# Attention and two MLPs on one core: attention units of blocks 3 to 7 eight ticks earlier, and the sums of x earlier in their cycle

## The chip, the cores and the metric

The program runs on one core of one Trainium2 chip. The metric is device time in microseconds (us) of a whole execution, inputs and outputs in HBM; a shorter time is better. Matrix products run on TensorE (PE), elementwise work on VectorE (DVE), ScalarE (ACT) and GpSimd (POOL). Most transfers are issued by SyncE (SP), in the order in which they are written.

## The reference

Linear attention with softmax over the features of q and over the sequence of k, then two MLPs without biases, all in float32.

```python
batch, heads, seq, dim = 8, 8, 576, 64      # 4608 tokens, d_model 512, d_ff 2048
q_s = softmax(q, axis=-1); k_s = softmax(k, axis=seq)
kv = einsum('bhsd,bhde->...', k_s, v)       # one 64 x 64 matrix for each head
x = einsum('bhsd,bhde->bhse', q_s, kv)      # then put in rows of 512 = heads x dim
h = x @ w_in;  x = (h * sigmoid(h)) @ w_out           # first MLP
h = x @ w_in2; out = (h * clip(h + 3, 0, 6) / 6) @ w_out2   # second MLP
```

## The kernel before

**Blocks, cycles, ticks.** Each MLP works on 9 blocks of 512 tokens: blocks 0 to 7 are the first 512 tokens of batches 0 to 7, block 8 is the 64 that are left of each batch. The hidden layer is cut in 8 chunks of 256 columns, so a block has 8 cycles, p = 0 to 7, and a cycle has 8 ticks, k = 0 to 7. `cycle(g)` writes one cycle of the first MLP for blocks 1 to 8 (g = 8 n + p): products 1 and 5, 6, 2 and 3, 7, then 4 of the block's operands with the chunk's weights, by a scheme with 7 products in place of 8, and between them the matmuls of the second layer for the chunk before (`G(0)` to `G(7)`, tiles y). Matmuls in float32r take a high and a low part of each operand, three to a product (L78 to L80). The weights of the first layer are read back from HBM into a ring of two tiles, 1.75 MB a cycle (L285).

**What DVE does in a cycle.** It adds `s2` (L780), which product 7 waits for; finishes A (L785) and B (L790, which product 4 waits for); forms the gate (L628) and the low part of its result (L75). On top come the attention's steps.

**Attention.** A batch has 4 units of two heads. The units of batch b are worked on beside block b - 1, by a table of ticks: `x_at(u)` is the tick of the unit's output x, and the list `plan` has all other steps at fixed distances: -28 `at_soft` (two DVE reductions, L374 and L377, then a POOL add, L379), -21 `at_spread` and `at_shift` (small transfers by SP), -20 `at_norm` (L421 to L424), -12 `at_tadd` and `at_sub` (POOL, L348 and L404), -4 `at_tmul` (POOL, L356), -3 and -1 the cast and the low part of q (L364, L368), -6 `at_kv` (five matmuls into bank D, then L482 on DVE), 0 and 2 the two halves of x (three matmuls each into bank D, which ACT copies into x at L514 and L516). Units are 16 ticks, two cycles, apart: the cycles with x alternate with those with kv.

**Operands of the next block.** When x of the next block is complete, `sums_x` (L549) forms four differences in two parts of two; in the last cycle, p = 7, `operand_x` splits seven operands, each a cast by ACT (L583) and a subtraction by DVE (L585). x lies in the tile xr, one buffer, of which `x_raw(n)` takes a new tile for each block. Block 8 has its x in the tile `rest`.

The order on each engine is the order in which the code is written (`manual_schedule`); the framework adds the waits.

Of the kernel before, what the change touches and what calls it, by code (L numbers as in the profile page):

```python
# [8 lines left out]
F32 = mybir.dt.float32  # L9
# [8 lines left out]
P = 128  # L18
NP = H // 2
TB = 512  # L20
NB = NT // TB
NF = DFF // P
KC = DM // P
# [6 lines left out]
NC = NF // 2  # L30
# [6 lines left out]
def attention_two_mlps(ctx: ExitStack, tc: tile.TileContext, kqT, kv5, qn, w1, w2, out):  # L37
# [7 lines left out]
    def stack(name, bufs, st, **kw):  # L45
        return st.enter_context(tc.tile_pool(name=name, bufs=bufs, reuse_waits="tile", **kw))

    tokens, weights_1, sums, attn = (ctx.enter_context(ExitStack()) for _ in range(4))
    x_p = stack("x", 1, tokens)
# [243 lines left out]
    def turned(u):  # L293
        return u >= TURNED * NP
# [227 lines left out]
    xr = {}  # L522
    tx = {}

    def x_raw(n):
        if n == NB - 1:
            return rest
        if n not in xr:
            xr[n] = x_p.tile([P, KC, TB], F32, tag="xr", name="xr")
        return xr[n]  # L530

    def first_x(c):
        k = c // 2
# [7 lines left out]
    def sums_x(n, part, add=nc.vector):  # L541
        x = x_raw(n)
        b11, b12, b21, b22 = (x[:, 2 * k:2 * k + 2, j * HT:(j + 1) * HT] for k in range(2) for j in range(2))
        if part == 0:
            t = z_p.tile([P, 2, 2, HT], F32, tag="z3", name="tx")
            tx[n] = t[:, 0], t[:, 1], z_p.tile([P, 2, HT], F32, tag="t4", name="t4")
        t3, t2, t4 = tx[n]
        for o, a, b in (((t3, b22, b12), (b12, b12, b11)), ((t2, b22, b12), (t4, b21, t2)))[part]:
            add.tensor_tensor(out=o, in0=a, in1=b, op=ALU.subtract)  # L549
# [129 lines left out]
    def at(tick, fn, *args):  # L679
        events.setdefault(tick, []).append((fn, args))  # L680

    def x_at(u):
        b, c = divmod(u, NP)
        return 22 + 10 * c if b == 1 else 64 * (b - 1) + 16 * c + 4

    for u in range(NP, NU):
        x = x_at(u)
        before = x_at(u - 2) if u - 2 >= NP else None
        if before is None:
            at(-90, at_load, u)  # L690
            at(-90, at_load_ev, u)
        elif turned(u):
            at(max(x - 42, 0 if turned(u - 2) else before - 11), at_load, u)
            at(x - 36, at_load_ev, u)
            at(x - 32, at_load_t, u)
        else:
            at(before - 5, at_load, u)
            at(before - 5, at_load_ev, u)
        if turned(u):
            plan = [  # L700
                (-28, at_soft), (-27, at_kexp), (-26, at_sendnm), (-26, at_send, "qm"), (-25, at_qexp),
                (-21, at_shift), (-21, at_spread, "qm"), (-20, at_knorm), (-20, at_norm), (-18, at_send, "qr"),
                (-12, at_tadd), (-12, at_sub), (-11, at_spread, "qr"), (-10, at_texp), (-9, at_exp),
                (-4, at_tmul), (-3, at_tcast), (-1, at_tlow),
            ]
        else:
            plan = [
                (-18, at_soft), (-17, at_kexp), (-15, at_qexp), (-14, at_trk, 0), (-13, at_knorm), (-13, at_norm),
                (-12, at_trk, 1), (-8, at_trq, 0), (-7, at_trq, 1),
            ]  # L710
        plan += [(-6, at_kv), (-4, at_kvsplit), (0, at_xhalf, 0), (2, at_xhalf, 1)]
        for d, fn, *args in plan:
            at(x + d, fn, u, *args)
# [9 lines left out]
    def cycle(g):  # L723
        A, B_, C = (banks[k] for k in "ABC")
        lo, hi = slice(0, HT), slice(HT, TB)
        m, t, p = place(g)
        n = m * NB + t
        last = p == NC - 1
        G = lambda k: layer_out(g - 1, k)
        late = g >= LATE  # L730
        early = n == 1 and NC - 4 <= p < NC - 2

        cast_out = split_out(0, p, lambda: raw_out[p])

        def side(k):

            run(8 * g + k)
            if n == 1:
                if early and k == 2:
                    pre.append(prepare_in(p + 2))  # L740
                if k < 2:
                    cast_out[k][1]()
                for i in {0: (3, 5), 1: (6,)}.get(k, ()):
                    if len(pre) and p in (NC - 3, NC - 2):
                        pre[0][i][1]()
                        if i == 6:
                            pre.pop(0)
                if early and k in (2, 3, 5, 6):
                    pre[-1][{2: 0, 3: 1, 5: 2, 6: 4}[k]][1]()
            if late and g > LATE and k < 4:  # L750
                pump({NC - 1: (1.2, 0.8, 0.8, 0), 0: (1.2, 1.2, 1.2, 0.7)}.get(p, (1.2, 1.2, 1.2, 1.2))[k], keep=True)
            if p == NC - 2 and k in (6, 7):
                sums_x(n + 1, k - 6)
            if last:
                for i in {1: (1,), 3: (5,), 4: (6, 2), 5: (3,), 6: (7,), 7: (4,)}.get(k, ()):
                    operand_x(n + 1, i)

        if g == LATE:
            attn.close()
            kept_p[1] = stack("kept1", 1, kept, side="right")  # L760
            m2_p.append(stack("m2", 1, right, side="right"))
            order = [*(q for q in range(NC) if q != STAYS), STAYS]
            stream.extend((1, q, 0) for q in order)
            feed(2)
            steps.extend(chain([second(q, 0) for q in order]))
        if g == PER - 1:
            pump(99)
            right.close()
            keep_in(3, 4, 4)
        product(g, 1, A[:, lo], True)  # L770
        nc.scalar.copy(B_[:, lo], A[:, lo])
        product(g, 5, C[:, lo], True)
        s5 = z_p.tile([P, HT], F32, tag="s5", name="s5")
        nc.scalar.copy(s5, C[:, lo])
        side(0)
        G(0)
        G(1)
        product(g, 6, B_[:, lo], False)
        s2 = z_p.tile([P, HT], F32, tag="s2", name="s2")
        nc.vector.tensor_tensor(out=s2, in0=B_[:, lo], in1=s5, op=ALU.add)  # L780
        side(1)
        product(g, 2, A[:, lo], False)
        product(g, 3, A[:, hi], False)
        G(2)
        nc.vector.tensor_tensor(out=A[:, hi], in0=A[:, hi], in1=s2, op=ALU.add)  # L785
        ba, bc = bend(g, 0, A), bend(g, 1, B_)
        next(ba)
        side(2)
        product(g, 7, B_[:, lo], False)
        nc.vector.tensor_tensor(out=B_[:, hi], in0=B_[:, lo], in1=s5, op=ALU.add)  # L790
        next(ba)
        G(3)
        side(3)
        G(4)
        product(g, 4, B_[:, lo], False)
        if not early:
            load_w(g + 2)
        for _ in ba:
            pass
        next(bc)  # L800
        next(bc)
        side(4)
        G(5)
        for _ in bc:
            pass
        side(5)
        G(6)
        side(6)
        G(7)
        side(7)  # L810
# [519 lines left out]
```

## Time and profile before

| what | value |
| --- | --- |
| median of 3 runs | 1656.68 us (1655.41 to 1660.07) |
| the profiled execution's own time | 1654.42 us |
| its span, first to last instruction | 1652.6 us |
| busy share: PE, weight loads, DVE, ACT, POOL | 97%, 88%, 72%, 46%, 15% |
| DMA traffic over the span | 382.95 MB, mean 232 GB/s |

The span lies 1.8 us under the execution's own time, and that time 2.3 us under the median of the runs. A busy PE is not a PE at its peak, since its matmuls are pipelined and their ends are modelled; a wait shows more surely in the length of a cycle, which is taken here from one first matmul of product 1 to the next. The first MLP's block 2 starts at 259.31, block 3 at 354.04, block 4 at 451.13, block 5 at 547.15, block 6 at 643.23 and block 7 at 736.89 us from the start of the span.

### The profile page before, as it was taken

The page shows a single profiled execution, that of the slowest core. Times are in us where ns is not written, and L with a number is a line of the kernel's source. Part 1 is how long each engine was busy: PE and PEld are TensorE (multiplying, and loading weights), DVE is VectorE, ACT ScalarE, POOL GpSimd, SP SyncE. Part 2 cuts the span into 40 slices and gives each one's busy share as a digit, 9 for nine tenths or more (in the row PEclk, how much of TensorE's full clock was granted, in tenths as well). Part 3 has the DMA queues.
Part 4 walks back from the last instruction along what each step waited for, and adds up shares of the span by engine and source line. Part 5 has one row for each costly group of instructions (what it writes and reads, how often), then busy time and mean ns, then how long its engine had stood idle before and what let it go on. Part 6 is the DMA issues. An engine that isn't in the chain of part 4 may idle for free.

```text
span 1652.6 us, 28084 instructions
## 1 busy us (share of the span) xinstructions
PE 1607.8 (97%) x11112; PEld 1450.8 (88%) x11112; DVE 1191.6 (72%) x1910; ACT 766.7 (46%) x1383; POOL 251.6 (15%) x188
## 2 busy tenths in 40 slices
PE   6999999999999999999999999999999999999998
PEld 4445878888889888898889999999999999999998
DVE  6999687575656657557777677777776587777775
ACT  5444555454544545444444555555554343333332
POOL 2211232221322222200000222222220000000000
PEclk9999999999999999999999999999999999999999
DMA  8589989999999999958897955555557943333332
GB/s 292 181 287 304 254 231 235 264 275 253 215 308 257 230 266 255 237 206 309 315 364 291 359 203 204 200 202 206 198 204 285 381 156 128 128 128 128 135 122 76
DMA packets 89419, 382.95 MB, mean 232 GB/s; under 512 B 21832, under 2 KB 25928, under 8 KB 67400
## 3 DMA queue, kind: packets, MB, share of 16 engines
q1 hardware_dynamic: 77128, 321.66, 62.5%
q10 hardware_dynamic: 12160, 59.51, 9.8%
q8 instruction: 87, 1.43, 0.4%
q14 instruction: 44, 0.36, 0.1%
HBM read 282.07 MB, written 99.06 MB: 231 GB/s over the span
## 4 chain that ended last, share of the span: by engine, by line
PE 67%; DVE 16%; DMA 9%; ACT 4%; issue 3%; POOL 0%; ACTq 0%; SPq 0%; DVEq 0%; POOLq 0%
PE M L1086 20%; PE y L78 5%; PE y L79 5%; PE y L80 5%; PE B L78 4%; PE B L79 4%; PE B L80 4%; PE A L78 4%; PE A L80 4%; PE A L79 4%; DMA ring<-wd 3%; DMA gd<-g 2%; DMA gt<-gd 1%; PE C L80 1%; PE C L79 1%
## 5 line engine op out<-in xcount | busy, mean ns | idle before, releaser
L1086 PE MATMUL M<-kout,f 128*128 128x256 f32 x2268 | 272.6, 281 | 0.9 <-DVE f L987 0.9
L1086 PEld LDWEIGHTS M<-kout,f 128*128 128x128 f32 x2268 | 270.4, 189 | 1.5 <-DVE f L987 1.1
L78 PE MATMUL y<-gs,woh 128*128 128x512 f32 x512 | 204.8, 400 | 0.0
L79 PE MATMUL y<-gs,woh 128*128 128x512 f32 x512 | 202.4, 395 | 0.0
L80 PE MATMUL y<-gs,wol 128*128 128x512 f32 x512 | 200.2, 391 | 0.0
L985 ACT CAST f<-gt 128x1024 fp32r<-128x1024 f32 x72 | 75.6, 1050 | 180.2 <-DVE gt L960 103.4
L78 PE MATMUL B<-o,ring 128*128 128x256 f32 x492 | 142.4, 289 | 13.6 <-DVE s L780 7.2
L75 DVE TENSOR_TENSOR gs<-g,gs 128x512 fp32r<-128x512 f32 x128 | 101.5, 793 | 62.4 <-ACT gs L74 61.8
L80 PE MATMUL B<-o,ring 128*128 128x256 f32 x492 | 139.1, 283 | 0.0
L79 PE MATMUL B<-o,ring 128*128 128x256 f32 x492 | 139.0, 283 | 0.0
L626 ACT ACTIVATE g<-A 128x512 f32<-128x512 f32 x72 | 43.0, 598 | 182.9 <-DVE A L785 166.2
L78 PE MATMUL A<-op,ring 128*128 128x256 f32 x444 | 126.7, 285 | 0.4 <-DMA ring<-wd 0.3
L79 PE MATMUL A<-op,ring 128*128 128x256 f32 x444 | 125.4, 282 | 0.4 <-DVE op L585 0.4
L80 PE MATMUL A<-op,ring 128*128 128x256 f32 x444 | 125.4, 282 | 0.0
L78 PEld LDWEIGHTS B<-o,ring 128*128 128x128 f32 x492 | 93.1, 189 | 33.7 <-DVE s L780 12.7
L74 ACT CAST gs<-g 128x512 fp32r<-128x512 f32 x128 | 79.1, 618 | 79.3 <-DVE g L628 76.7
L80 PEld LDWEIGHTS y<-gs,wol 128*128 128x128 f32 x512 | 96.5, 189 | 21.7
L987 DVE TENSOR_TENSOR f<-gt,f 128x1024 fp32r<-128x1024 f32 x72 | 88.0, 1222 | 30.7 <-ACT f L985 29.4
L78 PEld LDWEIGHTS y<-gs,woh 128*128 128x128 f32 x512 | 97.1, 190 | 12.7
L79 PEld LDWEIGHTS y<-gs,woh 128*128 128x128 f32 x512 | 97.3, 190 | 8.7
L78 PE MATMUL B<-o,kin 128*128 128x256 f32 x324 | 93.2, 288 | 7.3 <-DVE B L871 7.2
L854 DVE SCALAR_TENSOR_TENSOR g<-a,A 128x512 f32<-128x512 f32 x72 | 49.5, 688 | 69.2 <-ACT a L847 59.8
(228 smaller groups left out, 4210.0 us busy)
## 6 DMA issues: line engine op xcount, KB each, us to landing
ring<-wd SPq DMA_DIRECT2D x66, 1792.0 KB
gd<-g SPq DMA_DIRECT2D x72, 512.0 KB
gt<-gd SPq DMA_DIRECT2D x36, 1024.0 KB
st<-w_dram SPq DMA_DIRECT2D x16, 1024.0 KB
st<-w_dram ACTq DMA_DIRECT2D x16, 1024.0 KB
ev<-kv_dram SPq DMA_DIRECT2D x24, 640.0 KB
wd<-ring ACTq DMA_DIRECT2D x8, 1792.0 KB
kout<-wd SPq DMA_DIRECT2D x6, 1792.0 KB
```

What stands on the lines that cost most here:

```text
L74: nc.scalar.copy(hi, src)
L75: nc.vector.tensor_tensor(out=lo, in0=src, in1=f32(hi), op=ALU.subtract)
L78: nc.tensor.matmul(o, lhsT=wh, rhs=xh, start=start, stop=False, **kw)
L79: nc.tensor.matmul(o, lhsT=wh, rhs=xl, start=False, stop=False, **kw)
L80: nc.tensor.matmul(o, lhsT=wl, rhs=xh, start=False, stop=stop, **kw)
L626: nc.scalar.activation(out=a, in_=hb, func=AF.Tanh, scale=0.5)
L854: nc.vector.scalar_tensor_tensor(out=x["g"][:, j], in0=x["a", j], scalar=1.0, in1=x["AB"[j]], op0=ALU.min, op1=ALU.mult)
L985: nc.scalar.copy(o[0], src)
L987: nc.vector.tensor_tensor(out=o[1], in0=src, in1=f32(o[0]), op=ALU.subtract)
L1086: nc.tensor.matmul(M[:, h * 2 * P:(h + 1) * 2 * P], lhsT=a, rhs=b, start=p == 0 and h == 0 and e == 0, stop=p == NC - 1 and e == 2, skip_g ...
```

## The change

The units of batches 3 to 7 move 8 ticks, one cycle, earlier, and all their steps with them (`x_at`); those of batches 1 and 2 stay. The last unit's x is then written in cycle 5 and no longer in cycle 6, and the first unit's x of the batch after falls in the last cycle of the block before it. That needs x of two blocks in the tile xr at once, so `x_raw` hands out one tile throughout, and waits on it are by its regions. The sums of x go from ticks 6 and 7 of cycle 6 to ticks 2 and 5, in blocks 2 to 8; in block 1 they stay. Two loads get lower bounds, so that they do not come before their buffer is free.

```diff
     def x_raw(n):
         if n == NB - 1:
             return rest
-        if n not in xr:
-            xr[n] = x_p.tile([P, KC, TB], F32, tag="xr", name="xr")
-        return xr[n]
+        if not xr:
+            xr[0] = x_p.tile([P, KC, TB], F32, tag="xr", name="xr")
+        return xr[0]
...
-        return 22 + 10 * c if b == 1 else 64 * (b - 1) + 16 * c + 4
+        return 22 + 10 * c if b == 1 else 64 * (b - 1) + 16 * c + (4 if b == 2 else -4)
...
             at(max(x - 42, 0 if turned(u - 2) else before - 11), at_load, u)
-            at(x - 36, at_load_ev, u)
-            at(x - 32, at_load_t, u)
+            at(max(x - 36, before - 4), at_load_ev, u)
+            at(max(x - 32, before), at_load_t, u)
...
-            if p == NC - 2 and k in (6, 7):
-                sums_x(n + 1, k - 6)
+            if p == NC - 2 and k in ((6, 7) if n == 1 else (2, 5)):
+                sums_x(n + 1, int(k > 2 + 4 * (n == 1)))
```

**DVE at the end of block 3.** Before, from the end of cycle 6 into cycle 7: the four sums (L549, tiles tx, xr, t), the two reductions of a unit (L374, L377), then the cycle's own L780.

```order
L628 SCALAR_TENSOR_TENSOR g<-g,B 128x512
L75 TENSOR_TENSOR gs<-g,gs 128x512
L549 TENSOR_TENSOR tx<-xr 128x512
L549 TENSOR_TENSOR xr<-xr 128x2x256
L549 TENSOR_TENSOR tx<-xr 128x512
L549 TENSOR_TENSOR t_3935<-xr,tx 128x512
L374 TENSOR_REDUCE nm<-k 128x1
L377 TENSOR_REDUCE qm<-q 96x12
L780 TENSOR_TENSOR s_3978<-B,s_3956 128x256
L585 TENSOR_TENSOR op_1022<-xr,op_1022 128x512
L785 TENSOR_TENSOR A<-A,s_3978 128x256
L790 TENSOR_TENSOR B<-B,s_3956 128x256
```

Of the change, the same place from cycle 6's L780 on:

```order
L780 TENSOR_TENSOR s_3882<-B,s_3860 128x256
L785 TENSOR_TENSOR A<-A,s_3882 128x256
L549 TENSOR_TENSOR tx<-xr 128x512
L549 TENSOR_TENSOR xr<-xr 128x2x256
L790 TENSOR_TENSOR B<-B,s_3860 128x256
L628 SCALAR_TENSOR_TENSOR g<-g,A 128x512
L75 TENSOR_TENSOR gs<-g,gs 128x512
L628 SCALAR_TENSOR_TENSOR g<-g,B 128x512
L75 TENSOR_TENSOR gs<-g,gs 128x512
L549 TENSOR_TENSOR tx<-xr 128x512
L549 TENSOR_TENSOR t_3916<-xr,tx 128x512
L482 SCALAR_TENSOR_TENSOR kv<-D,kr,mask 128x128
```

Two sums now stand between L785 and L790 of cycle 6, the other two after its last L75; the reductions have gone to the start of cycle 6, and in their place at the start of cycle 7 stands the other unit's normalisation (L414 to L424).

**DVE in cycle 4 of block 1.** Before, from the normalisation of one unit on (wol and wi are weights that are still being prepared):

```order
L421 TENSOR_REDUCE qs<-q 96x12
L423 TENSOR_SCALAR qs<-qs 96x12
L424 RECIPROCAL qr<-qs 96x12
L780 TENSOR_TENSOR s_1594<-B,s_1562 128x256
L251 TENSOR_TENSOR wol<-wo,woh 128x1024
L785 TENSOR_TENSOR A<-A,s_1594 128x256
L192 TENSOR_TENSOR s<-wi 128x256
L192 TENSOR_TENSOR s<-s,wi 128x256
L790 TENSOR_TENSOR B<-B,s_1562 128x256
```

Of the change:

```order
L421 TENSOR_REDUCE qs<-q 96x12
L423 TENSOR_SCALAR qs<-qs 96x12
L424 RECIPROCAL qr<-qs 96x12
L374 TENSOR_REDUCE nm<-k 128x1
L377 TENSOR_REDUCE qm<-q 96x12
L780 TENSOR_TENSOR s_1599<-B,s_1561 128x256
L251 TENSOR_TENSOR wol<-wo,woh 128x1024
L785 TENSOR_TENSOR A<-A,s_1599 128x256
L192 TENSOR_TENSOR s<-wi 128x256
L192 TENSOR_TENSOR s<-s,wi 128x256
L790 TENSOR_TENSOR B<-B,s_1561 128x256
```

The two reductions of batch 3's first unit stand in cycle 4 now, ahead of L780; they stood at the start of cycle 5.

**PE at the end of cycle 6 of block 1.** Before, the second half of x of batch 2's last unit (L78 to L80 into D) and then G(7):

```order
L78 MATMUL D<-qh,kh 128x320
L79 MATMUL D<-ql,kh 128x320
L80 MATMUL D<-qh,kl 128x320
L78 MATMUL y_1199<-gs,woh 128x512
L79 MATMUL y_1199<-gs,woh 128x512
L80 MATMUL y_1199<-gs,wol 128x512
```

Of the change:

```order
L78 MATMUL D<-qh,kh 128x320
L79 MATMUL D<-ql,kh 128x320
L80 MATMUL D<-qh,kl 128x320
L473 MATMUL D<-ev 128x128 x4
L474 MATMUL D<-ev 128x128
L78 MATMUL y_1198<-gs,woh 128x512
L79 MATMUL y_1198<-gs,woh 128x512
L80 MATMUL y_1198<-gs,wol 128x512
```

The five kv matmuls of batch 3's first unit come right behind the x of batch 2's last, into the same bank D.

## Rows read from the trace of the kernel before

**Rows 1.** The page's first line: span and instructions.

```profile
span 1652.6 us, 28084 instructions
```

**Rows 2.** Busy time in stretches: blocks 2 to 5 of the first MLP.

```profile
core 0: us, PE busy (x) PEld busy (x) DVE busy (x) ACT busy (x) POOL busy (x), PEclk, DMA share, GB/s
259.31:354.04 94.73, 94.53 (x594) 83.96 (x592) 58.96 (x109) 45.74 (x97) 24.71 (x16) 1.00 0.98 261
354.04:451.13 97.09, 94.73 (x593) 84.11 (x592) 61.04 (x110) 46.48 (x98) 25.55 (x16) 1.00 0.97 253
451.13:547.15 96.02, 94.63 (x593) 83.83 (x592) 60.70 (x110) 46.33 (x98) 24.22 (x16) 1.00 0.98 257
547.15:643.23 96.08, 94.68 (x593) 83.95 (x592) 60.00 (x110) 46.20 (x98) 22.92 (x15) 1.00 0.98 257
```

**Rows 3.** The same view, single cycles: last and first ones of blocks, two undisturbed ones.

```profile
341.47:354.04 12.57, 12.49 (x77) 10.72 (x77) 10.06 (x14) 6.79 (x14) 6.68 (x4) 1.00 0.92 212
...
402.29:413.62 11.33, 11.33 (x74) 10.31 (x72) 6.13 (x14) 4.78 (x11) 2.17 (x2) 1.00 0.93 273
413.62:425.68 12.06, 12.06 (x78) 10.78 (x76) 6.96 (x11) 5.80 (x11) 6.15 (x4) 1.00 1.08 242
437.00:451.13 14.13, 12.59 (x77) 10.62 (x76) 11.63 (x15) 6.80 (x14) 6.29 (x4) 1.00 0.87 165
451.13:463.14 12.01, 11.69 (x73) 10.07 (x72) 10.49 (x23) 7.52 (x17) 0.00 (x0) 1.00 0.89 274
533.48:547.15 13.67, 12.60 (x77) 10.62 (x76) 11.16 (x15) 6.81 (x14) 5.09 (x4) 1.00 0.90 168
...
643.23:656.20 12.97, 11.65 (x74) 10.13 (x72) 11.46 (x23) 7.61 (x17) 3.11 (x2) 1.00 0.89 276
```

**Rows 4.** Waits of PE, 259 to 820 us: total, times, longest.

```profile
PE B L78 <- DVE s L780: 6.1, 8, 1.5
```

**Rows 5.** Timeline of PE at 442 us: start, duration, instruction, idle before.

```profile
444.29 0.38 PE L78 MATMUL B<-o,ring 128*128 128x256 f32 x1 [1.47 <-DVE s L780]
```

**Rows 6.** Timeline of DVE, 437 to 444 us, cycle 7 of block 3.

```profile
437.02 1.93 DVE L549 TENSOR_TENSOR tx<-xr 128x512 f32<-128x512 f32 x1
...
440.96 0.69 DVE L549 TENSOR_TENSOR tx<-xr 128x512 f32<-128x512 f32 x1
...
442.30 0.75 DVE L374 TENSOR_REDUCE nm<-k 128x1 f32<-128x576 f32 x1
...
443.82 0.41 DVE L780 TENSOR_TENSOR s<-B,s 128x256 f32<-128x256 f32 x1
```

**Rows 7.** Timeline of POOL: in cycle 7 of block 3, in cycle 1 of block 4.

```profile
436.48 1.92 POOL L348 TENSOR_TENSOR t<-t,qm 128x576 f32<-128x576 f32 x1 [12.14 <-DMA qm<-qm]
...
467.53 1.47 POOL L379 TENSOR_TENSOR q<-q,qm 96x768 f32<-96x768 f32 x1
```

**Rows 8.** Timelines of DVE and PE in the undisturbed cycle that starts at 413.62.

```profile
420.18 0.43 DVE L790 TENSOR_TENSOR B<-B,s 128x256 f32<-128x256 f32 x1 [0.97 <-PE B L80]
...
421.37 0.28 PE L78 MATMUL B<-o,ring 128*128 128x256 f32 x1
```

**Rows 9.** Stretches and a timeline of DVE: cycle 5 of block 1.

```profile
217.33:233.42 16.09, 14.13 (x77) 11.90 (x76) 13.04 (x19) 11.01 (x19) 7.02 (x3) 0.89 0.72 120
227.30:231.20 3.90, 3.73 (x12) 3.23 (x13) 2.88 (x7) 2.00 (x4) 0.00 (x0) 0.56 0.62 101
...
224.02 1.36 DVE L192 TENSOR_TENSOR s<-wi 128x256 f32<-128x256 f32 x1
```

**Rows 10.** Timelines of PE and ACT at the end of cycle 6 of block 1.

```profile
246.55 0.39 PE L78 MATMUL y<-gs,woh 128*128 128x512 f32 x1
...
247.02 0.22 ACT L516 COPY rest<-D 128x64 f32<-128x64 f32 x1
```

**Rows 11.** Timelines of DVE and PE in cycle 6 of block 7.

```profile
808.79 0.42 DVE L790 TENSOR_TENSOR B<-B,s 128x256 f32<-128x256 f32 x1
...
809.81 0.28 PE L78 MATMUL B<-o,ring 128*128 128x256 f32 x1
```

## The prediction, written before the changed kernel ran

> **What bounds the kernel now.** I read the page's first line, then busy time by block, then single cycles, then PE's waits, then the timelines around the longest wait. The span is 1652.6 us [rows 1], of an execution of 1654.42; the median of the runs stands 2.26 above that, so 2.3 is added to the sum at the end.
>
> In blocks 2 to 5 PE is busy for 94.5 to 94.7 us of 94.7 to 97.1 at full granted clock, DVE for about 60 [rows 2]. So PE sets the pace, with little left to win: some 1 to 2 us a block. The table of cycles says where. An undisturbed cycle takes 11.33 us with x and 12.06 with kv (the rows that start at 402.29 and 413.62). The last and the first of a block take more: the last cycle of blocks 2, 3 and 4 takes 12.57, 14.13 and 13.67, the first of block 4 12.01 and of block 6 12.97 [rows 3]. The rows of the same places that are not shown repeat these: the first cycles of blocks 3 and 5 lie within 0.03 of 12.01, the last of block 5 within 0.01 of 13.67. Against 12.06 the four last cycles lose 0.51 + 2.07 + 2 × 1.61 = 5.80, against 11.33 the four first ones 3 × 0.68 + 1.64 = 3.68; together 9.5 us.
>
> The cause is a late DVE. PE waits 6.1 us, 8 times, for L780 before product 7 [rows 4], once 1.47 [rows 5]. In that cycle DVE starts the four sums at 437.02, after the cycle has begun; the first takes 1.93 where a later one takes 0.69, and two reductions stand from 442.30 until L780 comes at 443.82 [rows 6]. POOL's L348 runs from 436.48 for 1.92 [rows 7], so a sum and a POOL operation overlapped and the sum lasted nearly three times as long.
>
> **The change part by part.** Kinds of work are neither added nor removed: the same sums, reductions and transfers run elsewhere.
>
> *The end of blocks 2 to 5.* The sums leave the start of cycle 7, the reductions too. In cycle 6 two sums, 2 × 0.69 = 1.38, stand ahead of L790. There DVE has waited 0.97 for PE, so L790 comes 0.41 later; it ended at 420.61 and product 4 read B at 421.37 [rows 8], 0.76 behind, so 0.35 are left. The other two sums follow the last L75, ahead of nothing due soon. In cycle 7 one unit's normalisation stands ahead of L780, as it does in other cycles that keep to 12.06. So all 9.5 us of stalls could go.
>
> *What DMA lets through.* Blocks 2 to 5 show DMA shares of 0.97 to 0.98 at 253 to 261 GB/s [rows 2]. Share times length gives 92.8, 94.2, 94.1 and 94.2 us of transfer time; a block of four kv and four x cycles would need 4 × 12.06 + 4 × 11.33 = 93.6 of PE. I take 94.2 as the least that blocks 3 to 5 can have. They gain then at most 97.09 - 94.2 = 2.9 (of which the stalls are 0.68 + 2.07 = 2.75), 96.02 - 94.2 = 1.82 and 96.08 - 94.2 = 1.88. With block 2's 0.51 and the 1.64 at the start of block 6, where the next block has no attention, that is 0.51 + 2.75 + 1.82 + 1.88 + 1.64 = **8.6**. The bounds: 9.5 if transfers spread better without the stalls, 0 if the shares mean that the ring of weights is the pace already.
> [...]
>
> *Block 1.* Its cycle 5 takes 16.09, that is 4.03 over 12.06: PE is idle 1.96 of it, and in 3.90 us behind that the granted clock is 0.56, which costs 3.90 × 0.44 = 1.7 [rows 9]. DVE's L192 takes 1.36 at 224.02 [rows 9], in the place where POOL's L379 stands behind the reductions. The reductions move into cycle 4, ahead of L780, L251 and the L192 of that cycle, so L379 meets weight preparation there just as well. Two ends: the pair of reductions, 1.52 (442.30 to 443.82) [rows 6], less 0.76 of room [rows 8], makes 0.8 of new stall while the old 4.03 goes (net -3.2); or the whole episode moves a cycle earlier and 0.8 comes on top (net +0.8). I take the upper end, as the same operations stand side by side, more of them than before. Then the kv matmuls come into bank D right behind the second half of x: PE went on at 246.55, and the ACT copy that empties D ended at 247.02 + 0.22 [rows 10], so PE waits 0.7 for it. Block 1 together: **+1.5**, between -2.5 and +2.
>
> *Blocks 7 and 8.* They have no attention beside them and no stall from it, but the sums come earlier as well. In block 7 L790 ends at 809.21 and product 4 starts at 809.81 [rows 11], 0.60 behind, with DVE full ahead of it. Two sums, 1.38, put it 0.8 late. Twice that is 1.6; block 7's last cycle loses its sums ahead of L780, from which I give back half of one: **+1.2**, between 0 and 1.6.
>
> *DMA issues.* Each unit's loads, its two small transfers by SP and the stores move with it by a cycle. In SP's queue they stand behind ring loads as before, the last yd store now behind the next one; nobody waits for yd before the second MLP. The price is nothing as long as the ring loads land early enough; otherwise it is the DMA rival below. The tile xr is now one, so a unit's x could wait for operands that still read the old block; ACT would wait then, and PE for D. All operands are formed in cycle 7 and x of the first unit is copied late in it, into other regions; I price it at 0 (with a bound of 0.7 a block, as for the wait in block 1).
>
> The sum: -8.6 + 1.5 + 1.2 = **-5.9**. Of 1654.42 that leaves 1648.5; with 2.3 to the median, **1650.8**, 0.36% less. A change under about 0.3%, 5 us, can't be told from none here; the bound lies at 1651.7.
>
> **The rivals.**
> A, the DMA gives it back. For it: the shares, and that the stalled cycles are those of the lowest rates (165 and 168 GB/s against 274 and 276 in the next, [rows 3]), so the queue may use the stall to catch up. Against it: full-rate cycles of 11.33 beside a share of 0.93. Blocks 3 to 5 gain about 0.6 each then, with 0.51 and 1.64: 4.0 of gain, 2.7 of loss, -1.3: 1655.4. Chance 0.12.
>
> B, block 1 pays more. For it: six DVE operations ahead of product 4 in cycle 4. If the episode costs 4.03 there and an L192 stall stays in cycle 5 as well, block 1 costs 4 rather than 1.5: -8.6 + 4 + 1.2 = -3.4: 1653.3. 0.05.
>
> C, no effect: the sums go, but operand casts and normalisation keep L780 late in cycles 7 and 0. For it: the p = 7 cycle has 15 DVE operations where an undisturbed one has 11 [rows 3]. Then only the waits of [rows 4] shift: 1656. 0.03.
>
> D, slower: the sums meet POOL. In cycle 6 the reductions now come first and L379 follows. It started 467.53 - 463.14 = 4.39 after its cycle's start and took 1.47 [rows 3, 7], to +5.86. The sums start where L785 ends, at about +5.6. If L379 starts later than some +4.1, the first sum overlaps it and takes about 1.93 as in [rows 6], and the second too if L348 follows; the pair takes 3.9 and L790 is 3.9 - 0.97 - 0.76 = 2.2 late in four blocks, 8.7 us, and each stall of 2 us may bring a stretch of lower clock as in [rows 9], 1.7 each, 6.8. Then -8.6 + 2.7 + 15.5 = +9.6: 1666. Against it: the overlap of 0.3 us is short, and only if the sum waits out or stretches by the whole operation does it hurt. 0.10.
> [...]
>
> E, better: block 1's episode goes for good, -3.2 + 0.7 = -2.5 in place of +1.5: 1646.8, and down to 1645 with the full 9.5 and none of the 1.2. 0.10.
>
> **How the numbers follow.** The likeliest, stalls gone and 1 to 3 us paid elsewhere, has 0.60 and its own range is 1647 to 1653.5; of that I put 0.45 below 1651.7 and 0.15 above. E adds 0.10 to faster; A, B and C add 0.20 to same; D is slower. Faster 0.55, same 0.35, slower 0.10. The range 1645 to 1657 leaves out D and the far edges of the rest.
>
> **What would show it.** Right: no wait of PE for L780 near 6.1 us in the stretch of [rows 4]; cycles 7 and 0 of blocks 2 to 6 at 12.1 and 11.4; cycle 6 not longer than 12.06; blocks 3 to 5 at 94.2 each. DMA the limit: PE waits for the ring, blocks at 95 or more. Block 1: a cycle 4 of 15 us or more and a cycle 5 near 12 is the moved episode; both near 12 is E. Blocks 7 and 8: PE waits for L790 in cycle 6, 0.8 us. D: sums of 1.9 in cycle 6 and L790 behind product 4. Wrong altogether would be a new wait in cycles that were clean before.

## The result, and the profile after

The changed kernel takes 1673.74 us (median of 6 runs, 1666.51 to 1676.62) against 1656.08 for the kernel before: ratio 1.0097, 95% interval 1.0077 to 1.0116. It is slower by 17.7 us; forecast were 5.9 less. The profiled execution took 1670.18, its span is 15.8 us longer than before's.

Its first line and its blocks 1, 3, 4, 5 and 7, in the columns of [rows 2]:

```profile
span 1668.4 us, 28080 instructions
...
155.20:265.28 110.08, 101.18 (x592) 84.89 (x591) 81.21 (x140) 58.50 (x113) 31.50 (x17) 0.98 0.89 239
...
360.11:455.15 95.04, 93.94 (x592) 84.40 (x593) 56.55 (x108) 45.89 (x97) 25.01 (x17) 1.00 1.00 265
455.15:556.58 101.43, 96.29 (x593) 86.13 (x592) 58.73 (x111) 46.21 (x98) 23.75 (x17) 0.97 0.94 243
556.58:654.47 97.89, 94.40 (x593) 84.19 (x592) 59.51 (x110) 46.51 (x98) 23.30 (x17) 1.00 0.97 251
...
748.43:840.91 92.48, 87.05 (x530) 77.09 (x528) 64.62 (x109) 40.67 (x69) 0.00 (x0) 0.98 0.80 302
```

Against before ([rows 2]; block 1 was 103.35 from 155.96, block 6 93.66, block 7 87.23 by their starts) block 1 loses 6.7, block 4 5.4, block 5 1.8, block 7 5.25; block 3 gains 2.05; the rest comes to 1.35 less. Single cycles show where, in the columns of [rows 3]:

```profile
231.78:253.11 21.33, 15.72 (x84) 12.78 (x83) 10.60 (x17) 8.60 (x18) 10.28 (x4) 0.92 0.69 185
443.82:455.15 11.33, 11.33 (x73) 10.31 (x72) 9.62 (x20) 6.34 (x14) 1.28 (x1) 1.00 0.94 272
455.15:468.68 13.53, 12.33 (x77) 10.71 (x76) 11.29 (x17) 7.84 (x17) 5.07 (x4) 1.00 0.88 168
...
492.07:507.50 15.43, 11.49 (x74) 10.12 (x72) 8.70 (x18) 4.70 (x12) 1.43 (x1) 0.94 0.84 229
748.43:764.30 15.87, 12.13 (x67) 10.76 (x66) 6.97 (x13) 5.42 (x11) 0.00 (x0) 0.89 0.66 248
```

These are cycle 6 of block 1, 7 of block 3, 0 and 3 of block 4, and 0 of block 7. Cycle 7 is clean, as forecast. But cycle 0 of block 4 now takes 13.53 (blocks 5 and 6: 13.57, 13.55) where a cycle with kv needs 12.06, and cycle 3 loses 4. PE's waits from block 2 to block 6, where the kernel before waits 5.8 us for L780 (in the longer stretch of [rows 4] it is 6.1, and 4.0 now):

```profile
PE A L78 <- DMA ring<-wd: 7.3, 6, 3.9
PE B L78 <- DVE s L780: 3.7, 3, 1.2
```

The waits for L780 fell, but now PE waits longest for the ring of weights, for which it hardly waited before. First cycle 0: DVE from the end of block 3 on, and POOL at the same time:

```profile
453.97 1.90 DVE L585 TENSOR_TENSOR o<-tx,o 128x512 fp32r<-128x512 f32 x1
455.79 2.06 DVE L585 TENSOR_TENSOR op<-xr,op 128x512 fp32r<-128x512 f32 x1
...
460.19 0.74 DVE L374 TENSOR_REDUCE nm<-k 128x1 f32<-128x576 f32 x1
460.85 0.93 DVE L377 TENSOR_REDUCE qm<-q 96x12 f32<-96x768 f32 x1
461.71 0.40 DVE L780 TENSOR_TENSOR s<-B,s 128x256 f32<-128x256 f32 x1
```

```profile
453.87 1.44 POOL L348 TENSOR_TENSOR t<-t,qm 128x576 f32<-128x576 f32 x1 [12.25 <-DMA qm<-qm]
455.26 2.03 POOL L404 TENSOR_TENSOR ev<-ev,nb 128x640 f32<-128x640 f32 x1
```

It is the picture of [rows 6] and [rows 7] one cycle later. Units are two cycles apart and the shift is one cycle: what stood in cycle 7 went to cycle 6, and the same steps of the next unit came from cycle 1 to cycle 0. So the next unit's L348 and L404 (L348 at 464.63 in cycle 1 of block 4 before) now meet two operand subtractions (1.90 and 2.06 for 0.68) in place of two sums, and its two reductions stand ahead of cycle 0's L780. Then the queue of SP, from cycle 0 to cycle 2 of block 4:

```profile
460.95 0.33 SPq L394 DMA_DIRECT2D nmd<-nm  x1
...
465.28 0.33 SPq L285 DMA_DIRECT2D ring<-wd  x1
469.51 0.33 SPq L667 DMA_DIRECT2D yd<-y  x1
...
472.10 0.60 SPq L316 DMA_DIRECT2D ev<-kv_dram  x1
472.86 0.34 SPq L335 DMA_DIRECT2D qr<-qr  x1
477.35 0.32 SPq L285 DMA_DIRECT2D ring<-wd  x1
...
486.08 1.09 SPq L344 DMA_DIRECT2D qr<-qr  x2
...
491.07 0.33 SPq L285 DMA_DIRECT2D ring<-wd  x1
```

SP waits for the reduction (nmd leaves 5.8 into cycle 0), the ring load follows at +10.1; the store of y (1 MB) and ev come next in the queue, and the small qr transfer (472.86) behind these. The store lands at 482.2, 12.7 us after its issue, and SP waits for the qr behind it until 486.08, 6.1 into cycle 2, and the ring load leaves 11.1 into it, where other cycles have 8.7. It falls into a stretch in which the k and q loads crawl (last two columns: DMA share, GB/s):

```profile
492.00:494.00 2.00, 2.00 (x16) 1.86 (x16) 0.95 (x2) 0.68 (x3) 1.33 (x1) 1.00 0.87 32
494.00:496.00 2.00, 2.00 (x15) 1.83 (x14) 1.54 (x6) 0.90 (x3) 0.10 (x1) 1.00 0.53 26
496.00:498.00 2.00, 2.00 (x17) 1.87 (x16) 0.93 (x3) 0.23 (x1) 0.00 (x0) 1.00 0.37 27
```

PE takes it up at 507.50, after the longest of the six waits for the ring, 3.94. Behind that wait the granted clock is 0.50 until 512, and cycle 4 takes 14.37 where 12.06 is clean: 2.3 us more.

### The profile page after: what moved, and what is told of

The parts are those of the page before. It is cut to its first block, busy times and chain, and to the rows that moved or that the text cites. A ratio compares the mean times of both kernels' runs of the same rounds, so it can differ in the third digit from the quotient of the medians.

```text
span 1668.4 us, 28080 instructions
## 1 busy us (share of the span) xinstructions
PE 1609.7 (96%) x11112; PEld 1452.8 (87%) x11112; DVE 1182.4 (71%) x1910; ACT 766.8 (46%) x1383; POOL 249.5 (15%) x188
## 4 chain that ended last, share of the span: by engine, by line
PE 63%; DVE 15%; DMA 14%; ACT 3%; issue 3%; SPq 0%; POOL 0%; ACTq 0%; DVEq 0%; POOLq 0%
PE M L1086 17%; DMA ring<-wd 8%; PE y L78 5%; PE y L79 5%; PE y L80 4%; PE B L78 4%; PE B L80 4%; PE B L79 4%; PE A L78 4%; PE A L79 4%; PE A L80 4%; DMA gt<-gd 3%; PE C L80 1%; PE C L79 1%; PE C L78 1%
## 5 line engine op out<-in xcount | busy, mean ns | idle before, releaser
L78 PE MATMUL y<-gs,woh 128*128 128x512 f32 x512 | 205.0, 400 | 0.0
L80 PE MATMUL y<-gs,wol 128*128 128x512 f32 x512 | 200.3, 391 | 0.0
L78 PE MATMUL B<-o,ring 128*128 128x256 f32 x492 | 141.3, 287 | 14.4 <-DVE s L780 4.9
L75 DVE TENSOR_TENSOR gs<-g,gs 128x512 fp32r<-128x512 f32 x128 | 98.0, 766 | 71.8 <-ACT gs L74 71.0
L80 PE MATMUL B<-o,ring 128*128 128x256 f32 x492 | 139.1, 283 | 0.0
L78 PE MATMUL A<-op,ring 128*128 128x256 f32 x444 | 127.4, 287 | 8.9 <-DMA ring<-wd 7.3
L80 PE MATMUL A<-op,ring 128*128 128x256 f32 x444 | 125.9, 284 | 0.0
L78 PEld LDWEIGHTS B<-o,ring 128*128 128x128 f32 x492 | 93.3, 190 | 31.1 <-DVE s L780 8.6
L80 PEld LDWEIGHTS y<-gs,wol 128*128 128x128 f32 x512 | 96.7, 189 | 21.8
L78 PEld LDWEIGHTS y<-gs,woh 128*128 128x128 f32 x512 | 97.2, 190 | 12.8 <-issue 0.2
L78 PE MATMUL B<-o,kin 128*128 128x256 f32 x324 | 93.2, 288 | 7.4 <-DVE B L871 7.4
L79 PEld LDWEIGHTS B<-o,ring 128*128 128x128 f32 x492 | 93.3, 190 | 7.1 <-issue 0.5
## 6 DMA issues: line engine op xcount, KB each, us to landing
ev<-kv_dram SPq DMA_DIRECT2D x24, 640.0 KB, 10.4
kout<-wd SPq DMA_DIRECT2D x6, 1792.0 KB, 12.5
```

Source lines behind the costliest of these rows:

```text
L75: nc.vector.tensor_tensor(out=lo, in0=src, in1=f32(hi), op=ALU.subtract)
L78: nc.tensor.matmul(o, lhsT=wh, rhs=xh, start=start, stop=False, **kw)
L79: nc.tensor.matmul(o, lhsT=wh, rhs=xl, start=False, stop=False, **kw)
L80: nc.tensor.matmul(o, lhsT=wl, rhs=xh, start=False, stop=stop, **kw)
```

## The experiments

Times are medians; ratios are to the kernel before, on the same chip, with their 95% intervals. Cycle lengths come from each run's own profile. Where a time is set against the changed kernel's 1673.74, two sessions are compared; the kernel before had medians from 1652.95 to 1657.54 in them.

**e1_again**: the changed kernel, unaltered. 

> The changed kernel once more, unaltered. If its losses are fixed by the order of the program, the same cycles are long again: cycle 6 of block 1 about 21 us, cycle 0 of blocks 4 to 6 about 13.5, cycle 0 of block 7 about 15.9, and some 7 us of waits for the ring in blocks 3 to 6, own time 1666 to 1677. What belongs to one execution alone is gone or elsewhere: of cycle 0 of block 7 (an issue of 5.3 us on the ACT queue) I expect that.


1666.83 us. Cycle 6 of block 1 19.78, cycle 0 of blocks 3 to 6 13.55 to 13.58, ring waits 4.5, and cycle 0 of block 7 15.42: this too came again. So all four losses belong to the program, though not their sizes: blocks 2 to 6 take 478.9 here and 483.2 in the profile above.

**e2_store**:

```diff
-            nc.sync.dma_start(out=yd[t], in_=o)
+            if 1 <= t <= 5:
+                at(NC * NC * (t + 1) + 16, nc.sync.dma_start, yd[t], o)
```

> The changed kernel with the store of y (1 MB a block) one cycle later in blocks 2 to 6, so that it stands ahead of qr, k and q as before, and no longer ahead of the spread of qm and of ev. If the store, in the cycle of ev, delays the small qr transfer, SP behind it and so the ring load of cycle 2, the waits for the ring (7.3 us) fall under 3 and the time by 3 to 6 us against the changed kernel, to about 1669. Rival: the transfers of the block are simply at their limit; then the ring waits stay at 6 to 8 and the time within 2 us.


1661.17 us, 1.0034 (1.0015 to 1.0054): 12.6 less than the changed kernel. No wait for the ring is left, though cycle 0 stays long (13.69, 13.08, 12.24, 13.53 in blocks 3 to 6). 5.3 of the 12.6 are the start of block 7, which is clean here (10.55) for a reason of its own (below).

**e3_soft**: the two reductions of cycle 0 behind L780.

```diff
-(-28, at_soft)
+(-27 if x % 64 == 28 else -28, at_soft)
```

> The changed kernel with the two reductions that stand at the start of cycle 0 one tick later, behind L780 instead of ahead of it. If DVE's late L780 makes cycle 0 of blocks 4 to 6 long (13.53, 13.57, 13.55), these fall to 12.1 to 12.4 and the time by 3 to 4.5 us, to about 1669.5; if the sends of the reductions then come later and the ring with them, part of it shows again as ring waits in cycles 2 to 4. Rival: the operand casts alone make it late; then cycle 0 stays over 13.


1677.90, 1.0127 (1.0103 to 1.0151). Cycle 0 is clean (12.09 to 12.13), and the time is longer. PE's waits of this kernel, block 2 to 6:

```profile
PE A L78 <- DMA ring<-wd: 13.5, 6, 3.6
```

The reductions come later, SP behind them, and the ring loses more than L780 gained. DVE's place alone doesn't cure it.

**e4_sums**: sums back at ticks 6 and 7 in all blocks.

```diff
-k in ((6, 7) if n == 1 else (2, 5))
+k in (6, 7)
```

> The changed kernel with the sums of x back at ticks 6 and 7 of cycle 6 in all blocks; the units stay a cycle earlier. If the new place of the sums brought the gain of cycle 7 (1.6 to 2 us a block in blocks 3 to 5), cycle 7 is about 1 to 2 us longer again and the time 3 to 6 us above the changed kernel. Rival: the shift of the units alone freed cycle 7, since no reductions stand there any more; then cycle 7 stays within 0.5 of 11.33, and blocks 7 and 8 gain up to 1 us: time 0 to 2 us below the changed kernel.


1671.48, 1.0082 (1.0059 to 1.0105). Cycle 7 of blocks 2 to 4 stays at 11.33, of block 5 at 11.53: the rival was right, the shift alone frees it. Cycle 6 of blocks 7 and 8 falls from 11.44 and 11.83 to 10.58 and 10.55, cycle 7 of block 7 rises from 10.55 to 11.52.

**e5_pad**: eight small ACT copies in block 6.

```diff
+            if g == 53:
+                pad = z_p.tile([P, 4], F32, tag="pad", name="pad")
+                nc.scalar.copy(pad, s5[:, :4])
```

> The changed kernel with eight ACT copies of 128 x 4 added in cycle 5 of block 6, whose results nothing reads. Nothing that cycle 0 of block 7 waits for is moved but the place of its instructions in ACT's code. If the 5.3 us issue at the start of block 7 (15.87, 15.42, 15.07 and 17.02 in four kernels with the same number of ACT instructions ahead of it) is ACT waiting for its next piece of code, cycle 0 of block 7 falls to about 10.6. Rival: the first use of the ACT queue is slow when the SP queue is in some state that the change brought; then it stays at 15 to 17.


1658.98 us, a single run; cycle 0 of block 7 11.25, 4.6 less. The reading is below, under the start of block 7.

**e6_mirror**: the kernel before with the store as in e2_store. 

> The kernel before with the store of y one cycle later in blocks 2 to 6, where it stands ahead of nb, qm and ev as in the changed kernel. If this order alone makes ring loads late, waits for the ring of 4 us or more come up in cycles 3 to 5 and the time goes up by 4 to 10 us to 1660 to 1666. Rival: the store is harmless there and the shift of the units needed too; then the time is within 2 us of before.


1655.12, 1.0005 (0.9988 to 1.0021). The rival holds: ring waits rise only to 1.8. There the store comes behind nb, qm and ev, not ahead, so it is no exact mirror. A later store costs little by itself in that order.

**e7_shift4**: e2_store with batch 3 unshifted, sums of block 2 at ticks 6 and 7.

```diff
-(4 if b == 2 else -4)
+(4 if b <= 3 else -4)
```

> The changed kernel with the store as in e2_store, and the shift only from batch 4 on: batch 3 keeps its ticks, and block 2 has its sums at ticks 6 and 7. The place where two units lie one cycle apart moves from block 1, which still prepares weights, to block 2. If that meeting makes cycle 6 of block 1 long (21.3, 19.8, 21.8), block 1 falls from 108 to 112 to about 103.5 and block 2 pays 1 to 3 us: time 1654 to 1656 against 1661 of e2_store. Rival: units one cycle apart cost as much anywhere; then block 2 rises by 5 or more and the time stays.


1660.71, 1.0032 (1.0012 to 1.0053). Block 1 is back at 100.10, and block 2, where the two close units now meet, takes 102.8 with these two cycles (5 and 6):

```profile
317.93:334.91 16.98, 12.27 (x77) 10.68 (x77) 5.80 (x14) 4.37 (x8) 2.94 (x2) 0.93 1.02 211
334.91:350.72 15.81, 15.23 (x83) 13.50 (x83) 8.54 (x13) 7.47 (x16) 7.23 (x5) 0.86 1.04 242
```

The rival was right: two units 8 ticks apart cost some 9 us without weights being prepared as well. The path is another, though. More than half is one wait for the ring at 334.91, the longest of this kernel:

```profile
PE A L78 <- DMA ring<-wd: 5.3, 2, 4.7
```

**e8_three**: e2_store, e3_soft and e4_sums together. 

> The changed kernel with the store as in e2_store, the reductions behind L780 as in e3_soft, and the sums back as in e4_sums. If e3_soft lost only because the ring had no room for sends that come later, and the store gives that room, cycle 0 of blocks 3 to 6 is 12.1 to 12.2 without new ring waits, 4 us less than e2_store, and blocks 7 and 8 gain 1 to 2: time 1655 to 1657. Rival: late sends cost ring time anyway; then ring waits of 4 us or more and 1660 or above.


1659.88, 1.0025 (1.0010 to 1.0040): cycle 0 12.1 to 12.3, but ring waits of 8.7, now in cycle 1 (13.95, 13.47, 13.03). The rival again.

**e9_early**: the reductions of cycle 0 earlier.

```diff
-(-28, at_soft)
+(-31 if x % 64 == 28 else -28, at_soft)
```

> The changed kernel with the two reductions of cycle 0 moved to tick 5 of cycle 7, ahead of three operand casts; the store stays where the change put it and SP's order is the same. DVE has as much ahead of L780 as in the changed kernel, but SP need not wait for the reductions in cycle 0. If it is this wait (nmd at +5.8 of cycle 0 in place of +4) together with the store right behind it that makes the ring late, the ring waits fall from 4.5 to 7.4 to under 3 and the time by 3 us or more, to 1670 or less. Rival: the store's place alone; then ring waits stay at 4.5 or more. POOL's L379 also comes ahead of L348 and L404: if these then run behind the casts, cycle 0 falls below 13.


1653.15, 0.998 (0.9964 to 0.9997): 20.6 less than the changed kernel by one edit, a shade below before; 5.3 of it is again the start of block 7 (10.55). Cycle 0 is 12.06, ring waits 3.5. POOL now has L379 ahead of L348 and L404, and the casts are done when these run. Block 4 of this kernel:

```profile
457.51:551.05 93.54, 93.54 (x593) 84.38 (x592) 55.78 (x110) 46.16 (x98) 24.81 (x16) 1.00 0.99 261
```

**e10_spread**: e7_shift4's store and e4_sums, the shift in steps of two ticks.

```diff
-(4 if b == 2 else -4)
+(4 if b == 2 else 2 - 2 * c if b == 3 else -4)
```

> The changed kernel with the store as in e7_shift4, the sums as in e4_sums, and the shift made in four steps of two ticks over the units of batch 3 (14 ticks apart), so that no two units lie 8 ticks apart. If the short distance is what costs (18 us more than e2_store's other blocks show in e7_shift4's block 2: 16.98 and 15.81), block 1 stays at 100 to 103 and block 2 at 94 to 97: time 1651 to 1655. Rival: steps at other ticks meet other work of the cycle, block 2 stays above 100, time 1658 or more.


1661.52, 1.0044 (1.0026 to 1.0062). Block 1 102.18, block 2 103.37, with cycles of 14.79 and 17.52: the rival. No two units lie 8 ticks apart here, and block 2 still pays 9.8 against e2_store's 93.6. (The 18 us of the expectation are 9: 102.8 against 93.6.) **e11_spread_early** adds e9_early's edit. 

> As e10_spread, with the reductions of cycle 0 earlier as in e9_early for batches 4 to 7. If POOL's two operations then leave the operand casts alone, cycle 0 of blocks 3 to 6 is 12.1 to 12.5 in place of 13.1 to 13.7 and the time 3 to 4 us below e10_spread; if not, within 1.5 us of it.


1655.73, 1.0001 (0.9986 to 1.0017): cycle 0 of blocks 3 to 6 is 12.06, 5.8 us less, and block 2 is still 106.4.

**e12_store_early**: e2_store and e9_early. 

> The changed kernel with the store as in e2_store and the reductions as in e9_early. Against e2_store (1661.2): 3 to 4 us less if cycle 0 is freed without new ring waits, the same if cycle 0 stays at 13 to 13.7.


1654.46, 0.9995 (0.9977 to 1.0013): 6.7 below e2_store, where 3 to 4 were expected. Cycle 0 is free and ring waits are 1.6, but cycle 0 of block 7 is 14.63 again.

**e13_pool**: nothing but two POOL operations of one unit a block, one tick later.

```diff
-(-12, at_tadd), (-12, at_sub)
+(d := -11 if x % 64 == 12 else -12, at_tadd), (d, at_sub)
```

> The changed kernel with two POOL operations (L348, L404) of one unit a block one tick later, so that they stand behind L379 in POOL's order and wait for the reductions; DVE's, PE's, ACT's and SP's orders are the same. If the cause of the long cycles 0 and, by SP's wait for the reductions, of the late ring is that these two meet the operand casts, the casts take 0.69 each, cycle 0 of blocks 3 to 6 is 12.1 to 12.4, ring waits fall under 4.5 and the time comes down to 1653 to 1659, as in e9_early. Rival: the place of the reductions on DVE; then cycle 0 stays at 13 or more and the time above 1665.


1653.44, 1.000 (0.9984 to 1.0017): 20.3 below the changed kernel, with the orders on PE, DVE, ACT and SP as they were. The same place on DVE, then on POOL, and cycle 0 of block 4:

```profile
457.83 0.68 DVE L585 TENSOR_TENSOR o<-t,o 128x512 fp32r<-128x512 f32 x1
458.43 0.75 DVE L374 TENSOR_REDUCE nm<-k 128x1 f32<-128x576 f32 x1
...
459.95 0.41 DVE L780 TENSOR_TENSOR s<-B,s 128x256 f32<-128x256 f32 x1
461.09 0.43 DVE L785 TENSOR_TENSOR A<-A,s 128x256 f32<-128x256 f32 x1 [0.73 <-PE A L80]
```

```profile
460.11 1.47 POOL L379 TENSOR_TENSOR q<-q,qm 96x768 f32<-96x768 f32 x1 [17.51 <-DVE qm L377]
461.54 1.43 POOL L348 TENSOR_TENSOR t<-t,qm 128x576 f32<-128x576 f32 x1
462.93 1.57 POOL L404 TENSOR_TENSOR ev<-ev,nb 128x640 f32<-128x640 f32 x1
```

```profile
455.93:467.99 12.06, 12.06 (x77) 10.78 (x76) 7.87 (x14) 7.58 (x17) 5.79 (x4) 1.00 1.05 194
```

The subtractions take 0.68 again, L780 waits for nothing though the reductions still stand ahead of it, and DVE is busy for 7.87 of the cycle in place of 11.29. Ring waits are 4.3, no clear fall (7.3 and, in e1_again, 4.5), so the store's order still costs something. Between the two profiles, which are 15.8 us apart, blocks 2 to 6 are 12.5 shorter, block 1 2, and the start of block 7 5.3, which is not this edit's doing (below); what comes before block 1 is 3.3 longer.

**e14_all** and **e15_all_store**: all batches from 2 on shifted, so that the close units meet in block 0. In both the first unit of batch 2 writes x into xr before all operands of block 1 are formed, so a part of the output comes from other rows; the work is the same in amount. 

> e9_early, with batch 2 shifted by 8 ticks as well, so that the two units that lie 8 ticks apart meet in block 0, and with the sums at ticks 6 and 7. If the short distance is what makes block 1 long (106 to 112 in the kernels with it there, 100 to 102 in those without), block 1 is 99 to 103, and blocks 2 to 8 as in e9_early: 1645 to 1649 if block 0 pays 0 to 2 us. Rival: block 0 pays the same 7 us or more, 1652 or above.


1661.10, 1.0046 (1.0026 to 1.0067). Block 1 takes 100.57, but it starts at 174.30 in place of 155.2: block 0 pays 15 to 19 us, the rival. 

> e14_all with the store of y a cycle later as in e2_store. If the store still costs ring time once the reductions are early (ring waits 3.5 in e9_early, 1.6 in e12_store_early), 1 to 2 us less than e14_all; otherwise within 1 us.


1669.32, 1.0090 (1.0070 to 1.0110), 8.2 more than e14_all: ring waits fall to 0.3 from 1.8, but cycle 0 of block 7 takes 15.37 (10.55 there) and block 1 starts at 178.9, 4.6 later.

**e16_before_pool**: the kernel before, with e13_pool's edit at x % 64 == 4. 

> The kernel before, with nothing but the same POOL edit as in e13_pool at the place where it applies there: L348 and L404 of one unit a block one tick later, behind L379, so that they no longer meet the sums of x at the start of cycle 7. If POOL's lock on the sums is the cause of before's long cycle 7 too (1.93 in place of 0.69, twice), cycle 7 of blocks 2 to 5 is 12.06 to 12.4 in place of 12.57, 14.13, 13.67 and 13.66, PE's waits for L780 fall from 7.2 to about 2.5 and the time by 4 to 5.5 us (0.25 to 0.33%), to 1650 against 1655. Rival: the two reductions, and the number of operations ahead of L780, make it late by themselves; then cycle 7 stays above 13 and the time within 2 us.


1662.46, 1.0046 (1.0028 to 1.0064): slower; both theories missed. DVE and POOL in cycle 7 of block 3:

```profile
443.11 0.69 DVE L549 TENSOR_TENSOR tx<-xr 128x512 f32<-128x512 f32 x1
...
445.96 0.41 DVE L780 TENSOR_TENSOR s<-B,s 128x256 f32<-128x256 f32 x1
446.63 4.39 DVE L585 TENSOR_TENSOR op<-xr,op 128x512 fp32r<-128x512 f32 x1 [0.26 <-ACT op L583]
```

```profile
446.12 1.47 POOL L379 TENSOR_TENSOR q<-q,qm 96x768 f32<-96x768 f32 x1 [17.94 <-DVE qm L377]
447.55 1.42 POOL L348 TENSOR_TENSOR t<-t,qm 128x576 f32<-128x576 f32 x1
448.93 1.53 POOL L404 TENSOR_TENSOR ev<-ev,nb 128x640 f32<-128x640 f32 x1
```

The sums take 0.69 and L780 is on time, as the first theory said; but POOL's three operations now run on end over the first operand subtraction, which takes 4.39, and L785 (at 450.94) and L790 come late behind it: cycle 7 is 14.5 to 16.1.

**e17_before_norm**: e16_before_pool with `at_knorm` and `at_norm` at -19 where x % 64 == 20. 

> e16_before_pool, with the normalisation of cycle 0 (L414 to L424) behind L780 instead of ahead of it. If it alone makes cycle 0 long by 0.65 to 1.64, that goes: 2 to 3.5 us less than e16_before_pool. Rival: as in e3_soft, the later step makes SP wait and the ring late; then the time is the same or longer, with ring waits of 2 us or more.


1658.92, 1.0030 (1.0015 to 1.0045). Cycle 0 of blocks 3, 5 and 6 falls to 11.87, 11.56 and 11.37 without ring waits, that of block 4 stays at 12.31: 3.5 less than e16_before_pool.

**e18_best**: e12_store_early, e4_sums, and two loads on another queue.

```diff
-            e = nc.scalar if m else nc.sync
+            e = nc.scalar if m and fed[0] > 18 else nc.sync
```

> e12_store_early with the sums at ticks 6 and 7 and with the first two weight loads of block 7 issued by SP instead of ACT. If the 2.7 to 5.4 us issue at the start of block 7 is ACT's, at the border of its code, it goes (cycle 0 of block 7 at 10.6 in place of 14.63), cycles 6 and 7 of blocks 7 and 8 take 0.9 to 1.3 less each, blocks 2 to 6 stay at 94, 94.5, 94, 94 and 91 and block 1 at 106 to 108: 4 to 6 us less than e12_store_early's 1654.5, so 1648.5 to 1650.5, below both kernels. Rival: ACT waits for its code in any case and L771 with it, or SP's queue delays these loads; then 1653 or more.


1650.56, 0.9960 (0.9938 to 0.9983): faster than both kernels. Blocks 1, 2 and 3:

```profile
155.86:267.33 111.47, 103.69 (x591) 87.99 (x591) 82.03 (x142) 59.40 (x115) 29.56 (x17) 0.94 0.92 235
267.33:360.91 93.58, 93.58 (x593) 84.35 (x592) 57.27 (x110) 46.22 (x98) 25.30 (x16) 1.00 0.99 258
360.91:454.48 93.57, 93.57 (x594) 84.36 (x593) 58.98 (x110) 45.97 (x98) 25.35 (x16) 1.00 1.02 268
```

Blocks 2 to 6 take 468.05 in place of before's 477.58: the 9.5 us that the shift can give are there. Block 1 still takes 8 of them back. The loads on SP and the sums of blocks 7 and 8 bring these two blocks back to what they were before (87.24 and 91.52; before 87.23 and 92.07). This profile's execution (1651.22) is 3.2 us shorter than before's (1654.42); the medians lie 7 apart, and no profile here shows where the rest is.

## Why the prediction was wrong, step by step

**What was right.** PE sets the pace, the waits for L780 at block ends were the loss to be had, and cycle 7 is freed (11.83, 11.33, 11.33, 11.33), by the shift alone: the new place of the sums added nothing to it (e4_sums). The signs named had the two kinds of cycle the wrong way round, since a shift by one cycle makes cycle 7 one with x (11.33) and cycle 0 one with kv (12.06). Blocks 7 and 8 cost what was said: cycle 6 longer by 0.89 and 1.28, cycle 7 of block 7 shorter by 0.98, together +1.2. PE's wait for bank D in block 1 was 0.9, forecast 0.7.

**The sum, term by term**, in the two profiles: blocks 2 to 6 +5.6 where -8.6 was forecast, block 1 +6.7 for +1.5, blocks 7 and 8 +6.0 for +1.2 (5.3 of it the start of block 7, below), and -2.5 ahead of block 1 and behind block 8; together the 15.8 of the spans.

**The step that failed first** is "So all 9.5 us of stalls could go". It followed the sums and the reductions out of cycle 7 and did not look at what the same shift brings into cycle 0: the next unit's reductions and POOL pair. There cycle 0 of blocks 4 to 6 lost 4.5, and the waits for the ring cost 7.3 and a stretch of lower clock. [rows 6] and [rows 7] had the cause, a sum of 1.93 beside L348; but the step treated it as a matter of the sums' place, when L348 and L404 come round with every unit. e13_pool and e9_early show that this one meeting is the larger part of the loss: without it the time is 20 us lower, about 5 of that from block 7. Rival D had this mechanism in the wrong place: it looked for POOL in cycle 6, with L379, and there it did not come (the sums of cycle 6 took 0.68 and 0.69).

**The DMA step** had the price at nothing while the ring loads come early enough, and as its worst case that the gain is given back (rival A). Its sign was bounded wrongly: the waits for the ring went from 0.3 to 7.3. Two things are shown to raise them, each by itself. One is the store's place ahead of nb, qm, ev and qr: e2_store moves it and has no wait, though cycle 0 is still late; e9_early and e13_pool leave it, with cycle 0 on time, and have 3.5 and 4.3; the four profiles with both (the changed kernel's, e1_again, e4_sums, e5_pad) have 4.5 to 7.4 (in e13_pool's block 4 the ring load leaves 8.7 into cycle 0, and 10.4 into cycle 2). The other is late reductions: e3_soft has 13.5, and e8_three, with the store moved, 8.7. In e8_three the ring loads leave on time, 8.7 to 8.9 into the cycle 0 of the three blocks that wait longest; why they land late was not found. A later store in the kernel before (e6_mirror), in another order, costs 1.8. The floor of 94.2 read from the DMA share was none: e9_early's block 4 takes 93.54 at a share of 0.99, e18_best's block 3 93.57 at 1.02.

**Block 1** was mis-sized, +6.7 for +1.5, and outside the range given. The episode of cycle 5 did shrink on moving (cycles 4 and 5 take 13.65 and 12.59, before 11.33 and 16.09 [rows 9]: 1.2 less, forecast 0.8 more). The loss is in cycle 6, 21.33 for 13.82 (0.7 of it the work of kv, which came in), of which no step looked at more than bank D. POOL's L356 of batch 2's last unit, before and in the changed kernel, and the two waits of PE that follow there:

```profile
225.39 1.40 POOL L356 TENSOR_TENSOR t<-t,qr 128x576 f32<-128x576 f32 x1 [0.29 <-ACT t L352]
```

```profile
235.19 5.45 POOL L356 TENSOR_TENSOR t<-t,qr 128x576 f32<-128x576 f32 x1 [14.96 <-DMA qr<-qr]
```

```profile
244.20 0.38 PE L79 MATMUL D<-ql,kh 128*128 128x256 f32 x1 [2.42 <-DVE ql L368]
...
247.66 0.41 PE L78 MATMUL D<-qh,kh 128*128 128x320 f32 x1 [1.56 <-ACT xr L514]
```

Before, it ran in cycle 5. The next batch's sends now stand ahead of its qr in SP's queue; it starts 10 us later, amid DVE's reductions and weight preparation, and takes 5.45; q's low part, x and the copies wait in turn. Behind these waits the granted clock is 0.52 for the last 3.1 us of the cycle. That the seam between unshifted and shifted batches is to blame is shown: with batch 3 unshifted (e7_shift4) or the seam elsewhere (e14_all) block 1 takes 100 to 101, and block 2 or block 0 pays 9 us or more. That it is the distance of 8 ticks is not shown: e10_spread has no such distance and loses as much in block 2. Nor is the path the same everywhere (in e7_shift4 it is mostly the ring), and in block 1 POOL's long operation and the late qr were not separated.

**The start of block 7**, 5.3 us, was in no step. ACT's timeline of the changed kernel:

```profile
748.40 5.32 ACTq L102 DMA_DIRECT2D st<-w_dram  x1
...
754.74 0.36 ACT L771 COPY B<-A 128x256 f32<-128x256 f32 x1 [4.41 <-issue]
```

The issue of a load holds ACT for 5.32 us, and PE waits 3.7 for L771. In the 19 profiles with this issue on ACT the length goes with the number of ACT's rows ahead of it in the trace: 956 or 957 rows 4.7 to 5.4 us, 959 to 963 2.7 to 3.5, 964 to 966 0.4 to 0.7, 951 and 947 0.4. An 8 KB packet of a DMA queue of the kind "instruction" starts 3.7 us after the issue here, which ends 1.6 us behind that start, and 3.6 before the issue in the kernel before. e5_pad's copies, which only change the code ahead, shortened the issue to 2.81, and e18_best, with the load on SP, has 10.55 for cycle 0. So 5 of the 17.7 us hang on this one issue on ACT. That ACT waits there for its next piece of code was the author's guess in the expectations of e5_pad and e18_best; what the issue waits for is not shown.

## What to carry to other kernels

When a step moves, list everything that belongs to it on every engine, and look up what stands at the place it goes to: a collision between two engines comes back there with the next unit's copy of the same step. Before pricing a transfer at nothing, follow the queue that issues it past each wait: here a reduction that came late held the issues behind it (nmd left 5.8 into cycle 0), and so did a 1 MB store put ahead of a small transfer that the queue waited for next (a ring load left 11.1 into cycle 2, where other cycles have 8.7). A change that brings in 9.5 us in five blocks can lose as much where the old and the new rhythm meet; look at that seam first.

## What the runs showed of the hardware that was not expected

DVE's L585, which has two inputs in SBUF, took longer beside POOL operations: 1.90 and 2.06 for 0.68 beside L348 and L404, and 4.39 beside three POOL operations on end (e16_before_pool). POOL's L356 took 5.45 for 1.40 amid DVE's work in cycle 6 of block 1. Each of the three L585 ended 0.56 us after the last POOL operation beside it had ended (455.87, 457.85 and 451.02, after 455.31, 457.29 and 450.46). L785, which reads PSUM, took 0.43 beside L379 in e13_pool. In the profiles of the kernel before and of the changed kernel, from 150 to 950 us, L780, L785 and L790, which all read PSUM, took at most 0.43 in 89 meetings with a POOL operation. L585 took at most 0.69 in the 104 cases without such a meeting; of the 24 with one, 13 took 1.05 to 2.06 and the other 11 at most 0.69. What sets the 13 apart is not shown.

From 492 to 498 us of the changed kernel, while small packets and the k and q loads were under way, DMA moved 26 to 32 GB/s, at shares of 0.37 to 0.87. The ring load issued at 491.07 moved its first packets after 498. Packets of the q load (3072 bytes) took 1.6 to 4.0 us on average between 490 and 496, and 0.14 between 498 and 500. And one DMA issue on ACT, the same in the source, took 5.32 us in the changed kernel, with 957 of ACT's rows ahead of it in the trace, and 0.37 in the kernel before, with 966.
